# A hand-ordered table stage: tables, projections and u issued in the order of the source

## The chip, the cores and the metric

The kernel runs on one core of a Trainium2 chip. A core has a matrix engine (TensorE, PE in the profile, with its weight loads as PEld), VectorE (DVE), ScalarE (ACT), GpSimd (POOL) and SyncE (SP), which here issues most DMAs. Each engine works through its own queue strictly in order, and the queues wait for each other by semaphores. The metric is the device time of one execution in microseconds.

## The reference

Two independent parts are computed and concatenated along the last axis: A, 32 heads of attention in a sliding window of 256 over 2048 tokens with 576 channels, and B, a diagonal state-space layer as a long convolution.

```
qkv = x @ wqkv                              # 2048 x 576 by 576 x 1728
p   = softmax(mask(q k^T * Dh**-0.5))       # 32 heads of 18, window 256
a   = (p v) @ wo

dt = exp(log_dt);  P = exp(dt*A*l)          # 576 channels x 128 states x 2048 taps
K  = real(sum over n of C*P*dt*B)           # the convolution's taps
y  = irfft(rfft(u, 4096) * rfft(K, 4096))[:2048] + u * Dskip
out = concat([a, y])
```

## The kernel before

The work falls into stages. A first one prepares parameters and the scales of the number formats. The second, the table stage, is where the change acts; it does three things side by side:

- **Projections** (`proj`, lines 182 to 252): x and wqkv are split into two float16 parts each, and every product is made of 14 matmuls (`mm14`, line 172). The scale of x comes from a maximum over all of x (`amax` over eight loaded pieces, then a reduction over the partitions on POOL in `pow2_max`, line 144). Then come four blocks of 512 tokens; each loads x again in two pieces (`load_rows`, lines 135 to 137), converts it on ACT and DVE (lines 226 to 230; the converted tiles `xh` and `xl` have one buffer each), multiplies out nine tiles for queries and keys (`m`, PSUM pool `pps`, three buffers) and four token tiles for values (`tk`), and stores them to DRAM.
- **Tables** (`tables`, lines 430 to 456): the taps K of the convolution are made from products of small tables of exponentials and sines. The 576 channels are 18 groups q of 32 (four sets of 8), and each group is two half groups c of 16 channels, 36 in all. For a group, `exps_ab` makes one table of exponentials (`mab`) and `factors` the sines and, on POOL, the factors A (lines 354 to 374). For a half group, `exps_q` makes exponentials (`mg`), `phases` an angle (an outer product on PE, then its fraction on ACT and DVE), `qtable` two sines on ACT and four products on DVE (Q, lines 404 to 408), `products` two tables on POOL (`m`, line 384), and `taps` contracts both on PE (line 422) into the tile `kp`, which ACT copies into K after every second half group. Outer products go through a PSUM pool `xps` of two buffers (line 314). Exponentials and sines need different tables in ACT, and a switch is an ACT_TABLE_LOAD; the exponentials of two groups stand together for that reason, every four half groups.
- **u** (`s1_u`, lines 470 to 477): the first step of the transform of u, 16 steps of four DMA loads, four pairs of matmuls in tiles of `pps` (line 466), four copies (`evac`: three of four on ACT, one on DVE) and two stores.

The three are Python generators. `merge` steps that one whose share of steps done is the lowest, so the source order is a fine mixture of the three: first 16 steps of `proj`, 20 of `tables` and 4 of `s1_u`, then 56, 304 and 12. In the kernel before, this source order is not yet the order of issue in the table stage: a planner works over it with its own costs, takes the source order as a priority, and sets the order of each engine's queue, matmul by matmul. It keeps the sequence of exponentials and sines as the source has it (`act`, line 331).

After the table stage `s1_k` transforms K in the same way (line 478), `att_setup` fills constant tiles with memsets (lines 588 to 606), and then attention and the convolution run together in the order of the source, under `manual_schedule` (line 991). Both stay as they are, but for memsets of `att_setup`.

Of the kernel before, what the change touches and what calls it, by code (L numbers as in the profile page):

```python
# [10 lines left out]
F32 = mybir.dt.float32  # L11
# [16 lines left out]
NQ = 18  # L28
# [49 lines left out]
def merge(*streams):  # L78
    live = [[g, n, 0] for g, n in streams if n]
    while live:  # L80
        s = min(live, key=lambda t: t[2] / t[1])
        try:
            next(s[0])
            s[2] += 1
        except StopIteration:
            live.remove(s)
# [16 lines left out]
class Kernel:  # L103
# [78 lines left out]
    def proj(self):  # L182
        nc, a, wp, dp, sp = self.nc, self.a, self.p["wq"], self.p["dram"], self.p["const"]
        self.qd = dp.tile([64 * 54 + 18, L], F16, name="qd")
        self.vd = dp.tile([8, 128, 16, 76], F32, name="vd")
        amx = sp.tile([128, 12], F32, name="amx")
        wr = self.p["K"].tile([128, 5, 1728], F32, name="K")
        for c in range(8):
            t = self.p["raw"].tile([128, 5, 256], F32, name="raw")
            self.load_rows(t, a["xT"], slice(c * 256, c * 256 + 256))  # L190
            self.amax(amx[:, c:c + 1], t)
            if c % 2 == 0:
                cs = slice(c // 2 * 432, c // 2 * 432 + 432)
                self.load_rows(wr[:, :, cs], a["wqkv"], cs)
            yield
        for c in range(4):
            self.amax(amx[:, 8 + c:9 + c], wr[:, :, c * 432:c * 432 + 432])
            yield
        px, self.sx = self.pow2_scale(amx[:, 0:8], "x")
        pw, self.sw = self.pow2_scale(amx[:, 8:12], "w")  # L200
        pz = self.pz = sp.tile([128, 1], F32, name="pz")
        self.esc = sp.tile([128, 1], F32, name="esc")
        nc.vector.scalar_tensor_tensor(pz, px, 0.25, pw, op0=OP.mult, op1=OP.mult)
        nc.vector.scalar_tensor_tensor(self.esc, pz, 18.0 ** -0.5, pz, op0=OP.mult, op1=OP.mult)
        wh = wp.tile([128, 5, 1728], F16, name="wh")
        wl = wp.tile([128, 5, 1728], F16, name="wl")
        for c in range(4):
            cs = slice(c * 432, c * 432 + 432)
            nc.scalar.activation(wh[:, :, cs], wr[:, :, cs], AF.Copy, scale=self.sw)
            nc.vector.scalar_tensor_tensor(wl[:, :, cs], wr[:, :, cs], self.sw, wh[:, :, cs],  # L210
                                           op0=OP.mult, op1=OP.subtract)
            yield
        self.K = self.p["K"].tile([128, 64, 144], F32, name="K")
        vst = [wp.tile([128, 32, 19], F32, name="vst%d" % i) for i in range(2)]
        for v in vst:
            nc.gpsimd.memset(v, 1.0)
        S = 2.0 ** -24
        for c in range(4):
            cs = slice(c * 512, c * 512 + 512)
            xh = self.p["x"].tile([128, 5, 512], F16, name="xh")  # L220
            xl = self.p["x"].tile([128, 4, 512], F16, name="xl")
            for hf in range(2):
                t = self.p["raw"].tile([128, 5, 256], F32, name="raw")
                self.load_rows(t, a["xT"], slice(c * 512 + hf * 256, c * 512 + hf * 256 + 256))
                h = xh[:, :, hf * 256:hf * 256 + 256]
                nc.scalar.activation(h, t, AF.Copy, scale=self.sx)
                nc.vector.scalar_tensor_tensor(xl[:, :, hf * 256:hf * 256 + 256], t[:, 0:4], self.sx, h[:, 0:4],
                                               op0=OP.mult, op1=OP.subtract)
                nc.vector.scalar_tensor_tensor(h[64:128, 4], t[64:128, 4], self.sx[64:128], h[64:128, 4],  # L229
                                               op0=OP.mult, op1=OP.subtract)  # L230
            yield
            for m in range(9):
                ps = self.p["pps"].tile([128, 512], F32, name="pp")
                self.mm14(ps, (wh, wl), (xh, xl), slice(m * 128, m * 128 + 128), slice(0, 512))
                st = self.p["pst"].tile([128, 2, 512], F16, name="qst")
                nc.scalar.activation(st[:, 0], ps, AF.Copy, scale=S)  # L236
                nc.vector.scalar_tensor_tensor(st[:, 1], ps, S, st[:, 0], op0=OP.mult, op1=OP.subtract)  # L237
                for e in range(2):
                    self.store_heads(st[64 * e:64 * e + 64], 2 * m + e, cs)
                yield  # L240
            for tk in range(4):
                v = vst[tk % 2]
                for hf in range(2):
                    ps = self.p["pps"].tile([128, 512], F32, name="pp")
                    w0 = 1152 + hf * 288
                    self.mm14(ps[:, :288], (wh, wl), (xh, xl), slice(w0, w0 + 288),
                              slice(tk * 128, tk * 128 + 128), flip=True)
                    nc.scalar.activation(v[:, 16 * hf:16 * hf + 16, 0:18],
                                         ps[:, :288].rearrange("p (h d) -> p h d", d=18), AF.Copy, scale=S)
                nc.sync.dma_start(self.vd[:, :, 4 * c + tk].rearrange("g p e -> p g e"),  # L250
                                  v.rearrange("p (g h) d -> p g (h d)", g=8))
                yield
# [175 lines left out]
            nc.scalar.activation(self.K[:, :, q * JJ:q * JJ + JJ].rearrange("p l j -> p j l"), kp, AF.Copy)  # L428

    def tables(self):  # L430
        self.mab, self.mg, self.AB, self.P, self.fr, self.Q = {}, {}, {}, {}, {}, {}
        yield from self.exps_ab(0)
        yield from self.exps_ab(1)
        yield from self.exps_q(0)
        yield from self.factors(0)
        self.products(0)
        self.phases(0)
        yield
        n = 2 * NQ
        for c in range(n):  # L440
            if c % 2 == 0 and c // 2 + 1 < NQ:
                yield from self.factors(c // 2 + 1)
            if c + 1 < n:
                self.phases(c + 1)
                yield
            yield from self.qtable(c)
            yield
            if c % 4 == 3 and c + 1 < n:
                if c + 5 < n:
                    yield from self.exps_ab(c // 4 + 2)  # L450
                yield from self.exps_q(c // 4 + 1)
            if c:
                yield from self.taps(c - 1)
            if c + 1 < n:
                self.products(c + 1)
        yield from self.taps(n - 1)


    def s1(self, src, g, l0, nl, pp):
# [9 lines left out]

    def s1_u(self):  # L470
        uv = self.a["u"].rearrange("(p l) (s j) -> s p l j", l=64, j=144)
        for l0 in range(0, 64, 4):
            ut = self.p["s1u"].tile([128, 4, 144], F32, name="ut")
            for st in range(4):
                self.nc.sync.dma_start(ut[32 * st:32 * st + 32], uv[st][:, l0:l0 + 4, :])
            self.s1(ut.rearrange("p l j -> p (l j)"), self.gx, l0, 4, "pps")
            yield

# [109 lines left out]
    def att_setup(self):  # L588
        nc, a, ap = self.nc, self.a, self.p["att"]
        self.ident = ap.tile([128, 128], F32, name="ident")  # L590
        nc.sync.dma_start(self.ident, a["c_id"])
        self.bias = ap.tile([128, 288], F32, name="bias")
        nc.vector.memset(self.bias, 0.0)
        for e in range(2):
            nc.sync.dma_start(self.bias[:, 256 * e:256 * e + 32], a["c_bias"][:, e])
        self.qb = ap.tile([128, 2, 32, 64], F16, name="qb")
        nc.gpsimd.memset(self.qb, 0.0)
        self.sets = []
        for b in range(3):
            d = {"Q": ap.tile([128, 2, HQ], F16, name="Q%d" % b), "K": ap.tile([128, 2, HK], F16, name="K%d" % b)}  # L600
            nc.vector.memset(d["Q"], 0.0)
            for h in (0, 64):
                nc.vector.memset(d["K"][h:h + 32], 0.0)
                nc.vector.memset(d["K"][h + 32:h + 64], -32768.0)
            self.sets.append(d)
        self.od = self.p["dram"].tile([2, D, L], F16, name="od")
# [341 lines left out]
    def build(self):  # L948
        nc, a = self.nc, self.a
        with ExitStack() as es:  # L950
# [9 lines left out]
            with ExitStack() as ek:  # L960
                self.pool(ek, "K", 1)
                with ExitStack() as e1:
# [8 lines left out]
                        self.pool(e1, n, b)  # L971
                    proj, tables, s1u = self.proj(), self.tables(), self.s1_u()
                    merge((part(proj, 16), 16), (part(tables, 20), 20), (part(s1u, 4), 4))
                    merge((proj, 56), (tables, 304), (s1u, 12))
                with ExitStack() as e1:
                    self.pool(e1, "s1s", 2)
                    self.pool(e1, "s1p", 3, PSUM)
# [50 lines left out]
```

## Time and profile before

| | |
|---|---|
| median of 3 runs | 1042.39 us (1042.09 to 1048.74) |
| the profiled execution | 1041.77 us, span 1040.1 us |
| preparation and scales | 0 to about 106 us |
| table stage | about 106 to 425 us |
| transform of K, memsets | about 430 to 479 us |
| attention and convolution | about 479 to 1040 us |
| PE busy over the span | 842.3 us (81%) |
| DVE, POOL, ACT busy | 703.1, 593.5, 569.9 us |

A line of groups reads: line of the source, engine, operation, what is written from what, shape, count | busy time in us, mean ns of one | idle time of the engine just before them, and what ended it. A line of waits reads: who waited for whom, total, times, longest. The chain is the work that ended last, followed back from the end; each piece has its start and its length. Tile numbers are left out: `pp` is a PSUM tile of projections or u, `x` one of the outer products, `r` a PSUM tile later on, and `mt`, `qst`, `vst`, `raw` are as in the source.

### The profile page before, as it was taken

The numbers are of one execution on the slowest core, as the hardware profiler recorded it, in microseconds if no ns is written. First come the engines' busy times: TensorE is split into PE (matmuls) and PEld (weight loads), VectorE is DVE, ScalarE is ACT, GpSimd is POOL, SyncE is SP. The second block draws the span as 40 slices with busy tenths as digits, with TensorE's granted clock in tenths as the row PEclk, the third lists the DMA queues.
The fourth block names the chain that finished last, engine by engine and source line by source line (L and its number), as shares of the span: only waits on it lengthen the run. The fifth ranks groups of instructions, "written<-read, shape, count | busy, mean of one in ns | idle before, by whom it ended". The sixth has DMA issues, their size and how long they took to land.

```text
span 1040.1 us, 26776 instructions
## 1 busy us (share of the span) xinstructions
PE 842.3 (81%) x10332; PEld 443.0 (43%) x10332; DVE 703.1 (68%) x1805; ACT 569.9 (55%) x883; POOL 593.5 (57%) x714
## 2 busy tenths in 40 slices
PE   1433998989799899865788888878888999987787
PEld 0212456446457457532343333333333444433345
DVE  2879374674765675464867788878878676767554
ACT  1784466666666666331266565556666565634470
POOL 0036495674676596301266776757776757664780
PEclk9956899999999999898899999999999999989999
DMA  9655544443454333587144465464544563579863
GB/s 271 182 169 154 133 108 102 113 99 84 124 114 106 79 89 92 135 257 218 48 126 136 130 209 157 147 177 129 158 124 146 144 184 113 152 175 240 222 185 124
DMA packets 155911, 152.27 MB, mean 146 GB/s; under 512 B 36856, under 2 KB 134392, under 8 KB 155592
## 3 DMA queue, kind: packets, MB, share of 16 engines
q1 hardware_dynamic: 148152, 131.98, 46.8%
q0 software_dynamic: 6128, 14.60, 5.5%
q10 hardware_dynamic: 1504, 3.99, 1.4%
q8 instruction: 81, 1.33, 0.6%
q14 instruction: 46, 0.38, 0.1%
HBM read 89.12 MB, written 61.01 MB: 144 GB/s over the span
## 4 chain that ended last, share of the span: by engine, by line
PE 40%; DVE 21%; DMA 12%; issue 10%; ACT 7%; POOL 7%; SPq 2%; DVEq 0%; ACTq 0%; POOLq 0%
PE pp L172 11%; PE r L641 4%; PE kp L422 4%; PE r L505 4%; PE po L705 4%; PE r L908 4%; DVE jk L648 3%; PE pp L466 3%; POOL P L693 3%; PE x L314 2%; DMA gk<-g 2%; PE ST L682 2%; DVE qb L632 2%; ACT P L684 2%; PE r L513 2%
## 5 line engine op out<-in xcount | busy, mean ns | idle before, releaser
L648 DVE CUSTOM_DVE_ANT_0 jk<-r,bias 128x288 f32<-128x288 f32 (+7 forms) x512 | 198.4, 433 | 96.8 <-PE r L641 95.9
L684 ACT ACTIVATE P<-ST,esc 128x1024 f32<-128x1024 f32 (+1 forms) x192 | 201.8, 1058 | 94.5 <-PE ST L682 93.5
L693 POOL TENSOR_SCALAR_AFFINE_SELECT P<-P 128x512 f32<-128x512 f32 x240 | 171.1, 741 | 107.0 <-ACT P L684 104.6
L384 POOL TENSOR_TENSOR m<-A,tr 128x1024 f32<-128x1024 f32 x72 | 145.6, 2045 | 86.8 <-PE kp L422 79.6
L641 PE MATMUL r<-K,qb 128*64 128x288 f16 (+7 forms) x1024 | 130.4, 297 | 38.3 <-DVE qb L632 11.2
L541 POOL TENSOR_TENSOR Y<-t,t 64x288 f32<-64x288 f32 x64 | 52.9, 826 | 119.8 <-DMA tk<-gk 59.8
L705 PE MATMUL po<-P,V 128*32 128x256 f32 (+2 forms) x1408 | 100.6, 397 | 16.9 <-ACT osb L713 8.1
L641 PEld LDWEIGHTS <-qb 128*64 128x64 f16 x1024 | 60.1, 109 | 121.3 <-issue 67.3
L422 PE MATMUL kp<-Q,m 128*32 128x64 f32 x4608 | 80.6, 224 | 16.5 <-issue 6.1
L422 PEld LDWEIGHTS kp<-Q,m 128*32 128x32 f32 x4608 | 70.4, 112 | 38.8 <-issue 26.6
L466 PE MATMUL pp<-ut,w 128*128 128x288 f32 x128 | 47.8, 506 | 42.6 <-DMA ut<-in_u_dram 25.4
L682 PE MATMUL ST<-Q,K 64*128 64x384 f16 (+2 forms) x704 | 73.8, 281 | 3.0 <-DMA Q<-mt 2.9
L325 DVE TENSOR_TENSOR k<-x,k 128x512 f32<-128x512 f32 (+1 forms) x54 | 33.9, 638 | 39.1 <-ACT k L324 39.0
L237 DVE SCALAR_TENSOR_TENSOR qst<-pp,qst 128x512 f16<-128x512 f32 x36 | 24.7, 685 | 50.6 <-ACT qst L236 42.4
L705 PEld LDWEIGHTS po<-P,V 128*32 128x32 f32 x1408 | 35.8, 110 | 51.4 <-issue 26.4
L542 POOL TENSOR_TENSOR Y<-t,t 64x288 f32<-64x288 f32 x64 | 54.4, 851 | 3.8
L172 PE MATMUL pp<-xh,wh 128*128 128x512 f16 x180 | 48.3, 391 | 9.4 <-DVE xh L229 6.5
L128 ACT ACTIVATE g<-pp 128x288 f32<-128x288 f32 (+1 forms) x84 | 34.1, 447 | 37.9 <-DMA gk<-g 20.0
L362 POOL TENSOR_TENSOR tr<-tr,mab 128x768 f32<-128x768 f32 x18 | 34.7, 1929 | 31.1 <-ACT tr L331 31.1
L466 PEld LDWEIGHTS pp<-ut,w 128*128 128x128 f32 x128 | 26.5, 227 | 58.2 <-ACT g L128 17.5
L172 PEld LDWEIGHTS <-wh 128*128 128x128 f16 x324 | 31.6, 99 | 45.7 <-issue 12.4
L505 PE MATMUL r<-tx,w 128*64 128x288 f32 x256 | 41.2, 439 | 10.7 <-DMA tx<-gx 9.5
(173 smaller groups left out, 1755.4 us busy)
## 6 DMA issues: line engine op xcount, KB each, us to landing
gx<-g SPq DMA_DIRECT2D x32, 288.0 KB
qd<-qst SPq DMA_DIRECT2D x72, 128.0 KB
gk<-g SPq DMA_DIRECT2D x16, 576.0 KB
tx<-gx SPq DMA_DIRECT2D x16, 576.0 KB
tk<-gk SPq DMA_DIRECT2D x16, 576.0 KB
h<-ho SPq DMA_DIRECT2D x16, 576.0 KB
raw<-in_xT_dram SPq DMA_DIRECT2D x16, 512.0 KB
Q<-qd SPq DMA_DIRECT2D x32, 216.0 KB
```

What stands on the lines that cost most here:

```text
L172: self.nc.tensor.matmul(ps, u, v, start=(i == 0), stop=(i == len(ops) - 1))
L384: self.nc.gpsimd.tensor_tensor(m, A[:, ch, a0:a0 + 8].unsqueeze(3).to_broadcast(sh), tr[:, ch, part, 0:8].unsqueeze(2).to_broadcast(sh), o ...
L422: nc.tensor.matmul(kp[32 * st:32 * st + 32, c % 2 * JJ2 + j, :], m[:, ch, a0:a0 + 32], Q[:, ch, term % 2, :], start=(term == 0), stop=(ter ...
L466: nc.tensor.matmul(ps, self.w1[:, part, :], src[:, o:o + k], start=True, stop=True)
L505: nc.tensor.matmul(ps[64 * par:64 * par + 64], w2[:, par, 64 * part:64 * part + 64], t[:, 2 * hs:2 * hs + 2, par, :], start=True, stop=True)
L542: nc.gpsimd.tensor_tensor(Y[par][64:128], t1[sl, 1], t2[sl, 1], op=OP.add)
L641: nc.tensor.matmul(ps[64 * b:64 * b + 64, :n], self.qb[:, b, t, :], d["K"][:, b, k0:k0 + n], start=True, stop=True, skip_group_check=True)
L648: nc.vector.tensor_tensor_reduce(out=jk[:, :n], in0=ps[:, :n], in1=self.bias[:, 288 - n:], scale=1.0, scalar=-3e38, op0=OP.add, op1=OP.max ...
L682: nc.tensor.matmul(ps[:, u, o:o + n], d["K"][h, jp, k0:k0 + 128], d["Q"][h, jp, q0:q0 + n], start=True, stop=True, skip_group_check=True)
L684: nc.scalar.activation(pt[:, 2 * jp:2 * jp + 2, lo:hi], ps[:, :, lo:hi], AF.Exp, scale=self.esc)
L693: nc.gpsimd.affine_select(v, v, pattern=[[0, 4], [sg, 128]], compare_op=OP.is_ge, fill=0.0, base=-1 if far else 0, channel_multiplier=-sg)
L705: nc.tensor.matmul(self.po[32 * j:32 * j + 32, t0 * 128:t1 * 128], V[:, kb * 76 + 19 * j:kb * 76 + 19 * j + 32], pt[:, j, o:o + (t1 - t0) ...
```

## The change

The second merge of the table stage is put under `manual_schedule`, so the source order is the order of each engine's queue there. The first merge stays with the planner. `tables` is written anew: in step c the phases of half group c + 2 come first, then the sines, Q and products of c + 1, then the outer product and fraction of the next factors (on even c), the taps of c, the rest of those factors, and the exponentials after every fourth half group. Before, the step of c had the factors and the phases of c + 1, then sines and Q of c, the taps of c - 1 and the products of c + 1. The matmuls, tables and numbers of steps are the same.

The loads of x for a block are issued after the second tile of the block before (for the first block, before wqkv's conversion), and those of u one step ahead. In `att_setup` the memset of rows 0 to 31 and 64 to 95 of the K tiles is dropped; the loads write those rows.

```diff
@@ proj
+        raws = []
+
+        def load(c):
+            for hf in range(2):
+                t = self.p["raw"].tile([128, 5, 256], F32, name="raw")
+                self.load_rows(t, a["xT"], slice(c * 512 + hf * 256, c * 512 + hf * 256 + 256))
+                raws.append(t)
+
+        load(0)
         for c in range(4):
...
-                t = self.p["raw"].tile([128, 5, 256], F32, name="raw")
-                self.load_rows(t, a["xT"], slice(c * 512 + hf * 256, c * 512 + hf * 256 + 256))
+                t = raws.pop(0)
...
+                if m == 1 and c < 3:
+                    load(c + 1)
                 yield
@@ tables
+        n = 2 * NQ
...
-        n = 2 * NQ
-        for c in range(n):
-            if c % 2 == 0 and c // 2 + 1 < NQ:
-                yield from self.factors(c // 2 + 1)
+        for c in range(-1, n):
+            if c + 2 < n:
+                self.phases(c + 2)
+                yield
             if c + 1 < n:
-                self.phases(c + 1)
-                yield
-            yield from self.qtable(c)
-            yield
-            if c % 4 == 3 and c + 1 < n:
-                if c + 5 < n:
-                    yield from self.exps_ab(c // 4 + 2)
-                yield from self.exps_q(c // 4 + 1)
-            if c:
-                yield from self.taps(c - 1)
-            if c + 1 < n:
-                self.products(c + 1)
-        yield from self.taps(n - 1)
+                yield from self.qtable(c + 1)
+                if c >= 0:
+                    self.products(c + 1)
+                yield
+            fa = self.factors(c // 2 + 1) if c % 2 == 0 and c + 2 < n else iter(())
+            if next(fa, 0) is None:
+                yield
+            if c >= 0:
+                yield from self.taps(c)
+            yield from fa
+            if (c + 1) % 4 == 3 and c + 2 < n:
+                if c + 6 < n:
+                    yield from self.exps_ab((c + 1) // 4 + 2)
+                yield from self.exps_q((c + 1) // 4 + 1)
@@ s1_u
-        for l0 in range(0, 64, 4):
+
+        def load(l0):
             ut = self.p["s1u"].tile([128, 4, 144], F32, name="ut")
             for st in range(4):
                 self.nc.sync.dma_start(ut[32 * st:32 * st + 32], uv[st][:, l0:l0 + 4, :])
+            return ut
+
+        nx = load(0)
+        for l0 in range(0, 64, 4):
+            ut, nx = nx, load(l0 + 4) if l0 < 60 else None
@@ att_setup
             for h in (0, 64):
-                nc.vector.memset(d["K"][h:h + 32], 0.0)
                 nc.vector.memset(d["K"][h + 32:h + 64], -32768.0)
@@ build
-                    merge((proj, 56), (tables, 304), (s1u, 12))
+                    with self.tc.manual_schedule():
+                        merge((proj, 56), (tables, 304), (s1u, 12))
```

## The prediction

> **What bounds the kernel now.** I read the stretches first, then the groups and the chain, then TensorE's waits. The stretches (start:end, length, busy of PE, PEld, DVE, ACT, POOL, granted clock, DMA share, GB/s):
>
> ```profile
> 97.00:105.80 8.80, 1.84 (x19) 0.70 (x20) 7.38 (x17) 7.39 (x10) 0.38 (x1) 0.63 0.06 11
> 105.80:424.90 319.10, 297.31 (x5492) 183.75 (x5491) 190.74 (x282) 198.32 (x355) 209.62 (x167) 0.98 0.44 104
> ...
> 429.50:478.95 49.45, 36.37 (x96) 17.89 (x96) 28.74 (x28) 16.13 (x36) 0.90 (x1) 0.95 0.76 227
> 478.95:1040.00 561.05, 471.08 (x4386) 221.41 (x4386) 407.67 (x1412) 297.71 (x421) 352.88 (x520) 0.97 0.56 155
> ```
>
> The new order acts on the second row: 319.1 us with PE busy for 297.3 and no other engine for more than 209.6. The 561 us of attention and convolution run the same code after it. The stage is bound by PE, so I ask first how little time its matmuls need. Steps from the chain and from PE's timeline (start, length), counts from the groups of this stage:
>
> ```profile
> 290.86 2.11 PE pp L466 x8
> ...
> 303.61 3.02 PE pp L172 x14
> ...
> 306.85 1.92 PE kp L422 x128
> ...
> 400.41 3.43 PE pp L172 x28
> ```
>
> ```profile
> 119.89 0.60 PE L314 MATMUL x<-c_cm,al 96*128 96x512 bf16 x2
> ```
>
> ```profile
> L422 PE MATMUL kp<-Q,m 128*32 128x64 f32 x4336 | 74.0, 221 | 7.3 <-issue 6.1 <-POOL m L384 1.2
> ...
> L466 PE MATMUL pp<-ut,w 128*128 128x288 f32 x88 | 27.0, 431 | 5.7 <-DVE qst L237 3.3 <-ACT g L128 2.5
> ...
> L314 PE MATMUL x<-c_cm,al 96*128 96x512 bf16 x63 | 22.7, 383 | 1.9 <-ACT mab L331 0.8 <-DVE k L325 0.6 <-ACT mg L331 0.2
> ...
> L314 PE MATMUL x<-c_ct,ps 96*128 96x512 bf16 x31 | 11.9, 383 | 0.0
> ...
> L314 PE MATMUL x<-c_ca,al 96*128 96x384 bf16 x12 | 3.7, 325 | 2.8 <-DVE k L325 2.8
> ```
>
> Projections: 36 tiles at 3.02 = 108.7 and 16 token tiles at 3.43 = 54.9. Taps: 4336/128 x 1.92 = 65.0. u: 88/8 x 2.11 = 23.2. Outer products: of 0.60 the second adds 0.22, so 94 wide ones are 20.7; 42 narrow ones (three groups of 15, 15 and 12, the last shown) at 384/512 of it are 6.9. Sum 279.4. The stage takes 39.7 more: 21.8 idle (319.1 - 297.3), 2% of clock = 6.4, and 11.5 that no record shows (changes between kinds, modelled ends that hide a bit of each wait). The named waits are many and short (total, times, longest):
>
> ```profile
> PE pp L172 <- DVE xh L229: 6.5, 2, 3.8
> PE kp L422 <- issue: 6.1, 5, 2.5
> ...
> PE pp L172 <- ACT xh L226: 2.8, 1, 2.8
> ...
> PE x L314 <- ACT mg L331: 0.2, 1, 0.2
> ```
>
> Ten rows, 27.9 us between 104 and 430. So a better order saves 30 us at the best; one that mixes PE's work less finely than the planner loses.
>
> **The start of the stage.** The chain before it:
>
> ```profile
> 85.64 0.37 SPq L135
> ...
> 86.61 3.32 DMA raw<-in_xT_dram
> ...
> 89.96 1.49 DVE amx L162
> ...
> 91.83 0.07 DVE xm L143
> ...
> 100.72 0.39 POOL xg L144
> ...
> 105.79 4.33 PE pp L172 x11
> ```
>
> The maximum over x is there at 91.9, its reduction on POOL runs at 100.7, behind table work. In the new source only the 20 first table steps lie ahead of it: it runs at about 92, the scale is ready at 93, and the second half of the first block (issued at 91.4 when its buffer is free, landing 4.3 later as the load above did, 85.64 to 89.94) is there near 96. The conversion on ACT is now the first step of the hand-ordered part; behind it on ACT wait the sines of half group 1 and the copies of u, and so u's fourth PSUM tile and PE. PE works steadily from about 97 instead of 105.8: 8.8 us gained (bounds 0, where the planner still holds the reduction back, and 12.8, where PE goes on as soon as the scale is there). But table work that ran in that gap now comes after it:
>
> ```profile
> L422 PE MATMUL kp<-Q,m 128*32 128x64 f32 x4608 | 80.6, 224 | 16.5 <-issue 6.1
> ```
>
> 4608 - 4336 = 272 tap matmuls are 4.1 us, some eight outer products 1.6, one u step 2.1 of which 1.6 still fits the gap: 6.2 more. The stage ends at 97 + 279.4 + 6.2 + 6.4 + 11.5 + X = 400.5 + X, with X the idle time of PE; before, at 424.9. Break-even is X = 24.4.
>
> **X, from the written order.** 304 table steps, 56 projection and 12 u steps are merged, so a projection tile stands whole after every fifth or sixth table step. Phases now run two half groups ahead of the taps, Q and products one, some 8 us (two buffers each, freed by taps that are past), so taps as a rule don't wait; on POOL the products stand ahead of the next factors, which they don't need. Three places remain. What they cost on the other engines:
>
> ```profile
> 99.85 0.67 ACT L331 ACTIVATE cs<-ab,halfpi 128x512 f32<-128x512 f32 x1
> 100.54 1.28 ACT L331 ACT_TABLE_LOAD   x1
> 101.83 0.49 ACT L331 ACTIVATE mab<-x 128x384 f32<-128x384 f32 x1
> 103.12 2.61 ACT L226 ACTIVATE xh<-raw,xr 128x1280 f16<-128x1280 f32 x2 [0.80 <-DVE xr L155]
> ```
>
> ```profile
> L331 ACT ACTIVATE mg<-x 128x512 f32<-128x512 f32 x64 | 35.8, 599 | 8.1 <-PE x L314 7.6
> ```
>
> ```profile
> L406 DVE TENSOR_TENSOR Q<-sn,mg 128x512 f32<-128x512 f32 x32 | 21.9, 685 | 16.9 <-ACT sn L331 16.6
> ```
>
> ```profile
> 87.90 1.81 POOL L362 TENSOR_TENSOR tr<-tr,mab 128x768 f32<-128x768 f32 x1
> ...
> 92.72 1.96 POOL L384 TENSOR_TENSOR m<-A,tr 128x1024 f32<-128x1024 f32 x1
> ```
>
> 1. *Eight exponential blocks* (two mab, eight mg). An outer product takes PE 0.22, its exponential on ACT 0.6, and there are two PSUM tiles; where the third product waits, the projection behind it waits. The block after taps 18: PE has a projection and two narrow products, 3.3 us; ACT waits 2.1 for DVE (four Q operations of 0.69 and the factors' fraction, less what ran beside PE's taps), has two sines 1.0, a copy 0.6, the table load 1.3 and mab 0.5 = 5.5: 2.2 lost, 0.6 more on the next two; then five products between projections cost 5 x 0.54 (ACT's step) less 5 x 0.22: 1.6. Together 4.4. So followed, the eight lie from 1.5 to 4.4, about 3.2 each; less 0.16 at each of three waits (hidden ends, in the 11.5), 2.7: 21.6. The planner had put single products inside projection tiles, hence 0.2 of mg waits in all. Bounds: 0 if ACT is always that far ahead, 6 each if its steps take full durations.
> 2. *Three conversions.* After taps 16 PE has 1.8 us (an outer product, three of u's four tiles; three PSUM tiles). ACT has sines 1.0, a copy 0.6, xh 2.6, sn and cs 1.2, then u's copy 0.35 that frees a tile: 5.7, so 3.9 lost. The others so: 4.2 and 2.7. 10 with hidden ends off, against 9.3 in the two rows above. Bounds 0 and 20.
> 3. *Factors to products on POOL.* 87.90 to 92.72 is 4.8 for the factors, then two products of 2.0: 8.8 behind ACT's sines, which stand behind Q on DVE. From the phases of half group 14 on, DVE has Q13 only after a projection's second half, at 4.8, and the factors' fraction at 8.0; sines at 8.7, POOL at 17.4. PE's work up to taps 14 (three projections, two taps, four outer products) is 14.2: 3.2 lost; elsewhere 0 to 1: 5 together. Filling at the start 3, the last half groups 2. Bounds 0 and 20.
>
> X = 21.6 + 10 + 5 + 5 = 41.6: the stage ends at 442.1, 17.2 later.
>
> **Loads and memsets.** Loading a block ahead brings nothing to x:
>
> ```profile
> L135 SPq DMA_DIRECT2D raw<-in_xT_dram x16: 367/376/587, 58.6 to 279.1; - x16
> ...
> L137 SPq DMA_DIRECT2D raw<-in_xT_dram x16: 518/595/599, 59.6 to 291.3; - x16
> ...
> L226 ACT ACTIVATE xh<-raw,xr x8: 1346/1362/1372, 103.1 to 342.2; 128x1280 f16<-128x1280 f32 x8
> ```
>
> Its last load was issued 50 us before its last conversion. On SP the new loads (six issues of 0.37 to 0.60) stand behind the second tile's stores, which wait for DVE, and ahead of the other tiles'; u's four stand a whole u step ahead. Stores behind them start 3 us later, and two buffers and the next tile's 3.0 us on PE cover that. Uncovered, a load costs PE the 4.3 above. The memsets that go:
>
> ```profile
> L603 DVE MEMSET K<- x6: 1125/1125/1125, 428.5 to 467.8; 32x1280 uint32 x6
> ```
>
> 6.75 us of DVE in the stretch from 429.5, whose DMA share is 0.76: between 0 and 6.75; I take 1, as PE is idle there for 13 of 49.5 us.
>
> Sum, against the profiled execution's own 1041.8 (span 1040.1): 1041.8 + 17.2 - 1 = 1058; it lies 0.6 below the median of 1042.4, so **1059**.
>
> **The clock.**
>
> ```profile
> 225.00:250.00 25.00, 21.92 (x351) 14.19 (x350) 10.27 (x15) 14.54 (x28) 9.61 (x10) 0.93 0.41 93
> ```
>
> ```profile
> 235.18 0.80 PE L466 MATMUL pp<-ut,w 128*128 128x288 f32 x2 [3.02 <-DVE qst L237]
> ```
>
> A stretch with one wait of 3.0 us had a clock of 0.93: 25 x 0.07 = 1.75 us lost beside the wait. If the 11 blocks and conversions each cost that, it is 19.3, less 6.4 counted: 1072. The Trainium skill, "TensorE: Matmul & The Clock Gate", section "HAM oscillation — how this bites in real kernels", says that waits above about 3.4 us throttle the clock again. By that rule only the conversions of 3.9 and 4.2 add a loss, 2 x 1.75 = 3.5, an estimate of 1062; the row, with a shorter wait, goes further than the rule.
>
> A second rule speaks against many changes between sines and exponentials. The Trainium skill, "ScalarE: Activation LUTs", section "What ACT_TABLE_LOAD costs", adds a drain of 1.38 us to each switch. By it the eight blocks would cost up to 11 us more, an estimate of 1070. The trace doesn't show it: the load at 100.54 takes 1.28, and mab starts at 101.83.
>
> **Rivals.**
> - *The half-group lead is enough* (faster). POOL and ACT have 110 and 121 us of slack in the stage, so ACT comes to each block ahead of PE (2 us are enough); only conversions wait, X = 10, and the clock loses 2 instead of 6.4: 406.1, 18.8 earlier, 1023. For it: the lead itself, and that POOL's long waits, all for taps, can go:
>
> ```profile
> POOL m L384 <- PE kp L422: 79.6, 10, 14.1
> ```
>
>   Against: the two PSUM tiles of the outer products, and ACT's sines behind Q.
> - *Nothing changes*: a wait in a block gives POOL and DVE time, places 2 and 3 vanish in it, X = 24.6: 1042. So too if the source order is nearly the planner's and the change doesn't do what it says; the x loads speak for that, the late reduction against.
> - *Everything queues*: full durations in the blocks (48), conversions twice (20), 10 for the rest: X = 78, 1095. Against: ACT is busy for 62% of the stage.
> - *The clock*, 1072.
>
> **Chances.** Forecast 0.38 (own range 1048 to 1074), lead 0.24, nothing 0.20, queues 0.12, clock 0.06. About 1% (10 us) is what a measurement tells here from no change: faster 0.24, same 0.20, slower 0.56. The range goes from 1020 (lead) to 1085, which leaves out most of the queues case and a tail of the lead.
>
> **What would show it.** Right: the first projection of the stage near 97 and the reduction near 92; the stage ends near 442 instead of 425, 345 us after that start, with some 42 us of idle time on PE, waits for mab, mg and u's copy on ACT at its head; 561 us after it unchanged. Wrong: a stage that ends before 415, PE idle there under 15 us, waits for mg under 5, or a stretch from tables to attention that moves by more than 5. A walk on eight blocks by mean steps is the weak point: half a microsecond each way per wait is 15 us.

## The result and the profile after

The changed kernel takes 1070.6 us (median of 4 runs, 1069.0 to 1072.8) against 1044.6 us before (4 runs, 1042.1 to 1048.7): 1.0247 times the time, 95% interval 1.0203 to 1.029. It is slower by 26 us; the forecast was 1059 in a range of 1020 to 1085.

The stretches of the changed kernel, cut at the first steady matmul of the table stage, at its last tap, at the first matmul on `tx` and at the end (columns as before):

```profile
0.00:104.35 104.35, 25.34 (x55) 11.86 (x56) 63.01 (x62) 46.41 (x54) 21.12 (x19) 0.71 0.66 185
104.35:465.00 360.65, 314.06 (x5795) 193.72 (x5795) 204.94 (x305) 208.99 (x373) 214.43 (x175) 0.96 0.39 94
465.00:517.00 52.00, 34.46 (x98) 16.88 (x98) 21.83 (x22) 17.22 (x37) 3.05 (x1) 0.95 0.87 251
517.00:1068.60 551.60, 467.77 (x4386) 220.54 (x4386) 406.06 (x1412) 298.13 (x421) 356.08 (x520) 0.98 0.54 156
```

The kernel before, cut at the same events:

```profile
105.80:428.40 322.60, 298.25 (x5512) 184.36 (x5511) 191.95 (x284) 198.32 (x355) 211.13 (x168) 0.98 0.44 104
428.40:484.30 55.90, 36.38 (x96) 17.90 (x96) 29.70 (x28) 17.16 (x37) 2.00 (x1) 0.90 0.78 227
484.30:1040.10 555.80, 471.08 (x4386) 221.41 (x4386) 407.67 (x1412) 297.71 (x421) 352.88 (x520) 0.97 0.55 154
```

The stage begins 1.45 us earlier and is 38.05 longer: PE's idle time in it grows from 24.4 (322.60 - 298.25) to 46.6 (360.65 - 314.06), its busy time by 15.8 (283 more matmul records, which had run ahead of the stage, and a clock of 0.96 instead of 0.98). The transform of K after it is 3.9 us shorter, attention and convolution 4.2. Together -1.45 + 38.05 - 3.9 - 4.2 = 28.5, the difference of the two spans.

PE's waits in the stage of the changed kernel (total, times, longest):

```profile
PE x L324 <- ACT mg L341: 10.2, 18, 2.2
PE x L324 <- ACT mab L341: 9.4, 6, 2.6
PE pp L479 <- ACT g L128: 8.8, 4, 4.7
PE kp L432 <- POOL m L394: 6.7, 6, 1.5
PE kp L432 <- issue: 4.9, 4, 2.6
PE x L324 <- DVE k L335: 1.9, 1, 1.9
PE pp L479 <- DVE qst L245: 1.5, 2, 1.1
PE pp L172 <- DVE xh L237: 1.4, 1, 1.4
```

44.8 us. The first two rows are outer products that wait for exponentials; before they made 1.0 us together (the row for mg stands in the prediction, that for mab is below). Of the third, 4.7 and 2.4 us are u's fourth tile behind the second and third conversion of x (PE goes on at 281.6 and 370.4); the other 1.7 stand away from the conversions, where u's copy is behind sines on ACT. The fourth are taps that wait for POOL's products.

```profile
PE x L314 <- ACT mab L331: 0.8, 1, 0.8
```

The chain ahead of the stage:

```profile
93.52 0.07 DVE xm L143
...
99.08 0.39 POOL xg L144
...
101.53 1.35 ACT xh L234
...
104.35 1.33 PE pp L479 x2
```

The reduction over the partitions again comes long after its operand, though no table work but the first products stands ahead of it. The conversion stands in front of sines and u's copy on ACT, and so PE does nothing for 33.0 us before the stage:

```profile
104.35 1.33 PE L479 MATMUL pp<-ut,w 128*128 128x288 f32 x2 [33.01 <-ACT g L128]
```

### The profile page after: what moved, and what is told of

Same layout as the page of the kernel before. It is cut to its first block, busy times and chain, and to the rows that moved or that the text cites. A ratio compares the mean times of both kernels' runs of the same rounds, so it can differ in the third digit from the quotient of the medians.

```text
span 1068.6 us, 26717 instructions
## 1 busy us (share of the span) xinstructions
PE 841.6 (79%) x10332; PEld 443.0 (41%) x10332; DVE 695.8 (65%) x1799; ACT 570.8 (53%) x883; POOL 594.7 (56%) x714
## 3 DMA queue, kind: packets, MB, share of 16 engines
q1 hardware_dynamic: 148152, 131.98, 44.8%
## 4 chain that ended last, share of the span: by engine, by line
PE 38%; DVE 18%; DMA 12%; issue 10%; ACT 9%; POOL 8%; SPq 4%; DVEq 0%; ACTq 0%; POOLq 0%
PE pp L172 10%; PE r L659 4%; PE kp L432 4%; PE r L524 4%; PE po L723 4%; PE r L926 4%; DVE jk L666 3%; POOL P L711 3%; PE pp L479 3%; DMA gk<-g 2%; PE ST L700 2%; PE r L532 2%; DMA K<-in_wqkv_dram 2%; ACT mg L341 2%; ACT P L702 2%
## 5 line engine op out<-in xcount | busy, mean ns | idle before, releaser
L702 ACT ACTIVATE P<-ST,esc 128x1024 f32<-128x1024 f32 (+1 forms) x192 | 201.9, 1059 | 94.0 <-PE ST L700 93.2
L711 POOL TENSOR_SCALAR_AFFINE_SELECT P<-P 128x512 f32<-128x512 f32 x240 | 173.4, 752 | 100.2 <-ACT P L702 97.9
L244 ACT ACTIVATE qst<-pp 128x512 f16<-128x512 f32 x36 | 21.4, 596 | 62.6 <-PE pp L172 51.9
```

Of the source, the lines that this page charges most:

```text
L702: nc.scalar.activation(pt[:, 2 * jp:2 * jp + 2, lo:hi], ps[:, :, lo:hi], AF.Exp, scale=self.esc)
L711: nc.gpsimd.affine_select(v, v, pattern=[[0, 4], [sg, 128]], compare_op=OP.is_ge, fill=0.0, base=-1 if far else 0, channel_multiplier=-sg)
```

## The experiments

Each kernel computes the whole reference. All ratios are against the kernel before, measured beside it (1042.2 to 1044.6 us).

| run | time, us | ratio | 95% interval |
|---|---|---|---|
| changed kernel | 1070.6 | 1.0247 | 1.0203 to 1.0290 |
| e1, planner | 1032.2 | 0.9883 | 0.9850 to 0.9915 |
| e2, hand order alone | 1177.8 | 1.1269 | 1.1228 to 1.1310 |
| e3, projections in five steps | 1064.3 | 1.0184 | 1.0143 to 1.0226 |
| e4, matmul for the maximum | 1067.7 | 1.0238 | 1.0194 to 1.0281 |
| e5, memsets alone | 1040.4 | 0.9972 | 0.9947 to 0.9997 |
| e6, old order of the steps | 1093.7 | 1.0478 | 1.0435 to 1.0520 |
| e7, conversion later, with matmul | 1091.2 | 1.0460 | 1.0417 to 1.0502 |
| e8, planner and matmul | 1031.4 | 0.9880 | 0.9845 to 0.9915 |
| e9, x loaded in place | 1085.9 | 1.0419 | 1.0364 to 1.0473 |
| e10, u loaded in place | 1147.9 | 1.0990 | 1.0950 to 1.1031 |
| e11, five steps and matmul | 1058.0 | 1.0146 | 1.0103 to 1.0190 |
| e12, conversion later, POOL | 1089.7 | 1.0448 | 1.0406 to 1.0491 |

My theory after the result: the hand order itself costs the time, because PE meets projection tiles whole between outer products and waits in the exponential blocks, at the conversions and at the start. The rivals: the new order of the steps, or the loads, cost it.

**e1: the planner back over the table stage.**

```diff
-                    with self.tc.manual_schedule():
-                        merge((proj, 56), (tables, 304), (s1u, 12))
+                    merge((proj, 56), (tables, 304), (s1u, 12))
```

> The changed kernel with the table stage given back to the planner: new order of the tables' steps, loads ahead, no memsets, but no hand order. Theory (the hand order of the queues costs the time, through PE's waits in the exponential blocks, at the conversions and at the start): within 1% of the kernel before, 1030 to 1050 us, waits for mg and mab under 3 us. Rival (the new order of the steps itself or the loads ahead cost it): 1060 or more.

Measured 1032.2 us, 38 below the changed kernel and 1.2% below the kernel before. PE's waits in the stage of this run:

```profile
PE kp L432 <- POOL m L394: 6.4, 6, 1.6
PE pp L479 <- ACT g L128: 4.0, 5, 1.3
PE pp L172 <- DVE xh L237: 3.7, 3, 2.5
PE pp L479 <- DVE qst L245: 2.0, 1, 2.0
PE x L324 <- ACT mab L341: 1.7, 3, 0.9
```

The waits for exponentials are nearly gone (no row for mg at all), those of taps for POOL stay as they were under the hand order. So the new steps, the loads ahead and the dropped memsets are a gain, and the hand order is what makes the changed kernel slow. PE's queue in this run has single outer products between the matmuls of a projection tile:

```profile
201.94 0.81 PE L172 MATMUL pp<-xh,wh 128*128 128x512 f16 x3
202.60 0.38 PE L324 MATMUL x<-c_cm,al 96*128 96x512 bf16 x1
202.82 0.59 PE L172 MATMUL pp<-xh,wh 128*128 128x512 f16 x2
```

The stage of this run, to be set beside that of the changed kernel:

```profile
106.00:425.30 319.30, 299.27 (x5529) 185.08 (x5527) 193.33 (x294) 201.71 (x362) 215.72 (x175) 0.97 0.44 104
```

It is 41.4 us shorter: PE is idle for 20.0 us in it (319.30 - 299.27) instead of 46.6, and busy for 14.8 less, since 266 of its matmul records stand ahead of the stage and the clock is 0.97. Of the kernels here this one and e8 are the fastest.

**e2, e6, e9, e10: what the hand order needs.** e2 is the kernel before with the one line of the hand order; e6 is the changed kernel with the old `tables`; e9 and e10 put the loads of x or of u back where they are used:

```diff
@@ e9
-        load(0)
...
-                if m == 1 and c < 3:
-                    load(c + 1)
...
+            load(c)
             for hf in range(2):
                 t = raws.pop(0)
@@ e10
...
-            ut, nx = nx, load(l0 + 4) if l0 < 60 else None
+            ut = self.p["s1u"].tile([128, 4, 144], F32, name="ut")
+            for st in range(4):
+                self.nc.sync.dma_start(ut[32 * st:32 * st + 32], uv[st][:, l0:l0 + 4, :])
```

> The kernel before with the hand order alone: old order of the tables' steps, loads and memsets as they were. Theory (hand order costs, the half-group lead gives part back): slower than the changed kernel, 1085 to 1130 us, since taps then stand right behind their products and wait for POOL. Rival (the lead brings nothing): 1065 to 1080, as the changed kernel.

> The changed kernel with the old order of the tables' steps: hand order, loads ahead and no memsets stay. Theory (the loads of u ahead are what the hand order needs most, 100 us or more of the 122.7 us of waits in the run with the hand order alone; the half-group lead is worth some 20): 1080 to 1100 us. Rival (the lead is worth most of it): 1120 or more. Second rival (the lead is worth nothing): within 5 us of the changed kernel's 1070.6.

> The changed kernel with x loaded where it is converted, as in the source before; u still one step ahead. Theory (under the hand order a load stands behind the stores of the block before on SP, and PE waits for it in full, 4.3 us and the queue): 3 conversions at 5 to 9 us more, 1085 to 1098. Rival (the load is hidden by taps and u): within 3 us of 1070.6.

> The changed kernel with u loaded in the step that uses it, as in the source before; x still one block ahead. Theory (u's loads stand behind stores that wait for projection tiles, 12 steps with 5 to 7 us each): 1130 to 1155, waits of PE for u 60 to 90 us. Rival (it was the old order of the tables that made u wait in the run with the hand order alone): under 1090.

Measured 1177.8, 1093.7, 1085.9 and 1147.9 us. From e2 to e6 the loads (and memsets) give back 84 us, from e6 to the changed kernel the half-group lead gives 23. Against the changed kernel, u in place costs 77 us and x in place 15. e2 was slower than its theory allowed (1085 to 1130), and by another wait than I had named. PE's largest wait in e10 and then in e2, both from 95 us on:

```profile
PE pp L479 <- DMA ut<-in_u_dram: 70.3, 10, 9.1
```

```profile
PE pp L466 <- DMA ut<-in_u_dram: 122.7, 12, 29.0
```

SP's queue in e10 shows why (start, length, count):

```profile
132.12 0.42 SPq L180 DMA_DIRECT2D qd<-qst  x1
132.64 1.79 SPq L488 DMA_DIRECT2D ut<-in_u_dram  x4
```

u's four loads leave right behind the last store of a projection tile, which had to wait for PE, ACT and DVE first; PE then has only what stands between in its own queue to do until the data land. Of e9, PE's waits in the stage:

```profile
PE pp L477 <- ACT g L128: 22.5, 5, 9.6
```

8.8 in the changed kernel, so 13.7 of the 15.3 us are here: a late x holds the conversion on ACT, u's copies stand behind it, and PE waits for u's fourth tile, not for x. That is 5.1 us for each of three conversions on the mean, at the lower end of what was expected.

**e3: projection tiles in five steps.**

```diff
@@ mm14
             self.nc.tensor.matmul(ps, u, v, start=(i == 0), stop=(i == len(ops) - 1))
+            if i in (2, 5, 8, 11):
+                yield
@@ proj
-                self.mm14(ps, ...)
+                yield from self.mm14(ps, ...)
@@ build
-                        merge((proj, 56), (tables, 304), (s1u, 12))
+                        merge((proj, 328), (tables, 304), (s1u, 12))
```

> The changed kernel with the 14 matmuls of a projection tile as five steps of the merge instead of one (328 projection steps in place of 56), so that PE has a few projection matmuls between any two outer products. Theory (whole tiles between outer products make PE wait): waits of PE for mg and mab fall from 19.6 us to under 8, the time falls by 8 to 16 us, to 1055 to 1063. Rival (ACT is the limit in the exponential blocks, wherever the tiles stand): waits as before, within 4 us of 1070.6.

Measured 1064.3, 6.3 us less than the changed kernel, just short of the 8 that the theory asked for. The waits it was made for, in the stage of this run:

```profile
PE x L326 <- ACT mab L343: 3.9, 4, 2.1
...
PE x L326 <- ACT mg L343: 1.6, 1, 1.6
```

5.5 us instead of 19.6, so ACT is not the limit in these blocks; the place of the tiles is. From the first conversion to the copy of the last taps the stage is 352.8 us (103.8 to 456.6) against 364.7 (100.3 to 465.0), 12 less. It is not the full 14.1 us of these waits, because others grew, those at the conversions above all (9.2 us for xh, 1.4 in the changed kernel). 3.5 of the 12 went at the front, where the scale came later in this run. In the profiled run another 5.4 went after the stage, where the code is the same (609.0 us from that copy to the end against 603.6).

**e4, e8, e11: a matmul in place of POOL's reduction of the maximum.**

```diff
-        nc.gpsimd.partition_all_reduce(g, m, 128, bass.bass_isa.ReduceOp.max)
+        if nm == "x":
+            mb = sp.tile([128, 128], F32, name=nm + "b")
+            nc.vector.tensor_copy(mb, m.to_broadcast([128, 128]))
+            ps = self.p["pps"].tile([128, 512], F32, name="pp")
+            nc.tensor.matmul(ps[:, :128], mb, self.idx, start=True, stop=True)
+            nc.vector.tensor_reduce(g, ps[:, :128], axis=AX.X, op=OP.max)
+        else:
+            nc.gpsimd.partition_all_reduce(g, m, 128, bass.bass_isa.ReduceOp.max)
```

`self.idx` is an identity, loaded at the start. e4 is the changed kernel with it, e8 the kernel of e1, e11 the kernel of e3.

> The changed kernel with the maximum over x reduced across the partitions by one matmul with an identity instead of POOL's reduction. Theory (POOL's reduction comes 5.5 us after its operand since POOL has to change its code behind the products): the scale is ready near 94 instead of 100, conversion, stage and end come 5 to 7 us earlier, 1063 to 1066. Rival (something else holds the conversion, the load of x or DVE): under 2 us, 1069 to 1072.

> The new order of the steps, loads ahead and no memsets, but the table stage given to the planner, and the matmul in place of POOL's reduction. Theory (the reduction's late start holds the conversion under the planner too, and the stage is bound by PE from there): 3 to 6 us below the run with the planner, 1026 to 1030. Rival (the planner had filled that time with table work of PE, so the end does not move): within 1.5 us of 1032.

> The changed kernel with the projection tiles in five steps and the matmul in place of POOL's reduction. Theory (the two gains, 6.3 and 2.9 us, lie in different stretches and add): 1060 to 1063, still slower than the kernel before. Rival (the finer mixture meets the same start and takes it up): 1064 to 1068.

Measured 1067.7, 1031.4 and 1058.0 us. In e4 the chain ahead of the stage is:

```profile
93.64 0.08 DVE xm L143
...
94.49 4.43 DMA raw<-in_xT_dram
...
99.02 1.36 ACT xh L241
...
101.86 0.75 PE pp L486 x2
```

The first half is converted at 96.4 instead of 100.3, but the second half of x lands only at 98.9, so the stage starts 2.5 us earlier: the load is the next limit. The median falls by 2.9, between the two theories; the runs of the two kernels overlap (1067.1 to 1074.3 and 1069.0 to 1072.8), so the earlier start is shown by the trace and not by the time. e11 takes off 6.3 more than e3, above what was expected. The two gains add, and part of it is e3's late front: the first conversion is at 97.0 instead of 103.8. It is still 1.5% slower than the kernel before, and 25.8 us slower than e1; what the planner does beyond these two was not taken apart. Under the planner (e8) the median falls by 0.8 us, within the spread of the runs, as the rival said. But in its profiled run, the fastest of its four, the copy of the last taps starts at 419.8 instead of 425.2 in e1, so whether the planner had filled that time stays open.

**e5: the memsets alone**, dropped from the kernel before.

> The kernel before without the six memsets, nothing else. Theory (they stand between the copies of K's transform on DVE and delay them): from the last tap to the first matmul on tx 52 to 53 us instead of 55.9, the time 2 to 4 us lower, 1038 to 1041. Rival (that stretch is held by its writes to DRAM): within 1 us of the kernel before.

Measured 0.9972 (0.9947 to 0.9997): 2.9 us. From the last copy of taps at 427.7 to `tx` at 481.7 it is 54.0 us instead of 55.9. The memsets stood among DVE's copies of that stretch.

**e7 and e12: the first conversion later.** With K's tile taken earlier, twelve table steps and one u step go ahead of the first conversion; e7 with the matmul for the maximum, e12 with POOL's reduction.

```diff
                     with self.tc.manual_schedule():
-                        merge((proj, 56), (tables, 304), (s1u, 12))
+                        merge((part(tables, 12), 12), (part(s1u, 1), 1))
+                        merge((proj, 56), (tables, 292), (s1u, 11))
```

> The changed kernel with the matmul in place of POOL's reduction, and with twelve table steps and one u step in the hand order ahead of the first conversion of x, so that ACT does their work while it would wait for the scale. Theory (33 us of idle PE ahead of the stage come from the conversion at the head of ACT's queue): taps 0 and 1 and one u step run before the scale is there, the stage ends 4 to 7 us earlier than with the matmul alone, 1060 to 1064. Rival (work moved ahead of the scale is given back in the stage, which waits elsewhere): within 2 us of the run with the matmul alone, 1066 to 1070.

> The changed kernel with twelve table steps and one u step ahead of the first conversion, POOL's reduction kept, so that PE's queue holds no wait for the maximum ahead of taps 0. Theory (the earlier run was slow because the matmul of the maximum blocked PE ahead of taps 0 and 1): taps 0 start before 95, 1068 to 1076. Rival (the later conversion and the other mixture of the steps cost it): 1080 to 1095.

Measured 1091.2 and 1089.7: both theories of e7 fell, and in e12 the rival held. In e7 the matmul for the maximum is ahead of the taps in PE's queue, so PE waits 22.6 us for its operand there. e12 has no such wait; PE's queue:

```profile
90.90 3.64 PE L433 MATMUL kp<-Q,m 128*32 128x64 f32 x128
...
101.24 0.44 PE L433 MATMUL kp<-Q,m 128*32 128x64 f32 x8 [6.16 <-DVE Q L416]
...
115.31 0.66 PE L433 MATMUL kp<-Q,m 128*32 128x64 f32 x16 [4.46 <-POOL m L395]
117.22 3.22 PE L433 MATMUL kp<-Q,m 128*32 128x64 f32 x112 [1.26 <-POOL m L395]
120.37 2.30 PE L172 MATMUL pp<-xh,wh 128*128 128x512 f16 x5
```

Taps 0 do run at 91, but the first projection starts at 120.4, 11 us later than in the changed kernel (109.2). The conversion, now on ACT behind sines that wait for DVE, starts 5.2 of these later (105.5 and 100.3), and the taps that now stand ahead of the projection wait 5.7 for POOL. The stage ends at 480 instead of 465, 15 us later, although 256 more tap matmuls have run by the first projection. So the other mixture of the steps costs time after it too: PE waits 25.6 us for exponentials (19.6 in the changed kernel) and 17.8 for POOL's products (6.7). Why was not taken apart.

## Why the prediction was right, and where it was off

**Direction and sum.** Slower was forecast with 0.56, and 1059 against 1070.6 is 12 us low. The stage was to end 17.2 later; by the last taps it ends 36.6 later (428.4 to 465.0). What follows it took 8.1 less (3.9 and 4.2) where I had 1. The 19.4 of the stage are 7.35 at its start, 8 of clock and 5 more of idle PE (46.6 for 41.6), 20.4 together. That the time came out only 12 low is luck, since the 7.1 behind the stage went the other way.

**X nearly held, by its largest part.** Predicted 41.6 us of idle PE in the stage; the named waits make 44.8, the idle time 46.6. Exponential blocks 21.6: measured 10.2 + 9.4 = 19.6, and e3 shows that the whole tiles between outer products cause them. Conversions 10: measured 4.7 + 2.4 for u's fourth tile, the place I gave, and 1.4 for xh, 8.5, at the second and third; at the first, u's tile did not wait. POOL's products 5: 4.0 of the row of 6.7. Start and last half groups 3 and 2: 0.6 at 119.0, and 2.6 (1.2 at 459.3 and 1.5 at 463.1), the rest of that row. What the walk did not have are 9.5 us: the rest of the rows of "issue" (162.2 to 192.3) and the row of DVE's fraction (382.0), 6.3 together, 1.7 for u's tile away from the conversions, and 1.5 for `qst`. That the total came so near is partly luck, since the walk's own bounds were wide.

**The start failed.** The step was "it runs at about 92, the scale is ready at 93", with PE steady from 97 and 8.8 us gained. Measured: the reduction at 99.1, PE from 104.35, 1.45 gained; 7.35 us of the miss. Table work that now runs after the start was sized right: all 4608 tap matmuls stand in the stage. I had put the reduction's lateness down to table work ahead of it on POOL. POOL's own rows, of the kernel before and then after, say otherwise:

```profile
92.72 1.96 POOL L384 TENSOR_TENSOR m<-A,tr 128x1024 f32<-128x1024 f32 x1
100.72 0.38 POOL L144 PARTITION_ALL_REDUCE xg<-xm  x1 [6.04 <-PE x L314]
108.28 1.94 POOL L384 TENSOR_TENSOR m<-A,tr 128x1024 f32<-128x1024 f32 x1 [7.18 <-issue]
```

```profile
82.10 9.85 POOL L394 TENSOR_TENSOR m<-A,tr 128x1024 f32<-128x1024 f32 x4
99.08 0.38 POOL L144 PARTITION_ALL_REDUCE xg<-xm  x1 [7.14 <-issue]
```

Products end at 91.95, and 7.1 us pass before the reduction, with its operand there at 93.6; before, 6.0, and 7.2 again until the next product. The profile puts the 6.04 down to a product of PE, but a gap of 6.15 at the same place in e5 to DVE, and the 7.14 to nothing; the length stays and the name changes. The row of 7.18 stood in the trace before I predicted. The Trainium skill, "GPSIMD Engine Reference", section "2.1 Instruction dispatch", gives about 6 us for the first call after new code is loaded into POOL, with nothing to see in the profile; the three gaps of 6.0 to 7.2 agree with it. e4 took the reduction away, and the stage started 2.5 us earlier, no more, since the load of x's second half ends at 98.9 (I had said near 96).

**The clock was undersized.** 6.4 us in my sum; 4% of 360.65 is 14.4, 8 more. The rival that priced the clock at 13 us more by rows came nearer than the forecast did. In slices of 5 us from 110 to 465, the clock of the changed kernel is below 1.00 at seven places, and each follows one of its seven longest waits of PE. One of these waits and the slice behind it, columns as above:

```profile
168.41 0.76 PE L324 MATMUL x<-c_cm,al 96*128 96x512 bf16 x2 [1.98 <-ACT mab L341]
```

```profile
170.00:175.00 5.00, 4.70 (x24) 2.92 (x22) 0.00 (x0) 1.11 (x3) 2.55 (x2) 0.66 0.01 2
```

The seven waits are 1.98 to 4.70 us long. The places lose 13.6 us in all (the length of each slice times what its clock lacks of 1.00), 1.7 behind each wait and 3.4 around the longest. That is what the clock rival said of each wait. By the rule of waits above some 3.4 us, in the Trainium skill's "TensorE: Matmul & The Clock Gate", section "HAM oscillation — how this bites in real kernels", only one of them would count; the trace doesn't agree, with six drops behind waits of 1.98 to 2.64. Length alone doesn't decide: in the kernel before, waits of 3.02 and 3.81 us were followed by a loss of 1.7 each, one of 2.69 (at 350.0) by none. That the waits cause the lower clock is an inference from this order in time; it fits the runs, with a clock of 0.88 for 103.7 us of idle PE in the stage of e10 and 0.99 for 21.4 in that of e8, but no run varied single waits.

**Loads: right for the kernel before, undersized for the hand order.** "Uncovered, a load costs PE the 4.3 above": for x it is 5.1 by e9, for u 6.4 for each of 12 steps by e10 (77 us), since the load stands behind stores that wait. And "loading a block ahead brings nothing" holds only where the planner moves loads ahead by itself.

**Memsets.** 1 us of a bound of 6.75; e5 gives 2.9, with an interval from 0.3 to 5.5.

**Attention and convolution** were to stay at 561 us from their start; from the first matmul on `tx` they took 551.6 instead of 555.8. The run with the hand order alone has 550.5 there (1171.7 - 621.2) with the memsets in, e5 without them 554.3 (1036.0 - 481.7). So neither the memsets nor the new tables explain it. Over all runs, whose code there differs by the memsets alone, this stretch takes 550.5 to 557.5 us (e7: 1089.5 - 532.0), so the 4.2 lie within what it varies by; what varies it stays open.

**Rivals.** The lead was not enough: ACT reached the exponential blocks late in spite of 152 us of idle time in the stage (360.65 - 208.99). "Nothing changes" through the loads held for x only under the planner. That everything queues (1095) is near what the old order of steps gives under the hand order (1093.7).

## What to carry to other kernels

Before an order written by hand replaces a planner's, check at which grain the planner mixes: here it set single outer products inside a group of 14 matmuls, and a source that could only mix whole groups made PE wait 20 us at that place. Mixing these groups finely as well gave back 12 us in the stage, 6 in the whole time. Look on the queue that issues the DMAs first: a load that stands behind stores in the source waits for what these stores wait for, and moving it one step ahead was worth 77 us. And try the parts of a change alone: the new steps under the old planner were 1.2% faster than the kernel before, hidden behind a line that cost 38 us.

## What the runs showed of the hardware that I had not expected

Between POOL's last product and its reduction lie 5.8 to 8.1 us in all the runs here that keep the reduction, and 6.8 to 7.4 from the reduction to the next product where nothing else held it (the kernel before, e1, e5), on an engine that shows as idle. The granted clock of a stage that is 87% busy (314.06 of 360.65) was 0.96, with losses of 1.7 us behind single waits of 2.0 to 2.6. A table load on ACT in the middle of its work showed nothing beyond its 1.28 us.
